# Keys loaded in two layouts and the decay moved to the values, in the attention stage of a fused attention and expert kernel

## The chip, the cores and the metric

The kernel runs on one core of one Trainium2 chip, in one launch. The metric is the device time of that launch in microseconds, the median of several runs. Its engines are named as in the profile: PE is TensorE (PEld its weight load), DVE is VectorE, ACT is ScalarE, POOL is GpSimd, and SP is SyncE, whose queue issues most transfers.

## The reference

Three layers follow each other: an attention without softmax, in which a score decays with the distance of its two positions, a choice of one of 8 experts for each token, and a dense layer with a cosine.

```python
# q, k, v: 8 batches, 8 heads, 576 positions, 64 columns, float32
scores = scale * np.matmul(q, k.transpose(0, 1, 3, 2))
gamma = 1.0 - 2.0 ** (-5.0 - np.arange(H))            # one for each head
Dmat = np.where(rel >= 0, gamma[:, None, None] ** rel[None], 0.0)   # rel = query position - key position
attn = np.matmul(scores * Dmat[None], v)              # rows of all heads side by side: x, 4608 x 512
...
logits = x @ w_gate                                   # 8 experts, the largest is taken
h = np.maximum(xe @ w1[e], 0.0); ye = h @ w2[e]       # for the tokens of each expert
...
h = x @ w_in; g = h * np.cos(h); out = g @ w_out      # 4608 x 512, 2048 wide inside
```

## The kernel before

The change lies in the attention stage, the first 180 us or so. It works through 40 steps: 8 batches, each of which is cut into 5 chunks of positions, four of 128 and a last one of 64. Since gamma to the power of a distance is a product of one power for the query and one for the key, the kernel multiplies each row of keys by gamma to the minus position (`decay_k`, tile `kp`) and each column of results by gamma to the position (the table `gx`).

Each step `i` issues, in this order: the transposes of the decayed keys of a chunk ahead (`transposes`, PE into `tp`, ACT copies them to `kpT`); the scores of chunk `i` (`scores`, PE into `sc`, DVE multiplies them by the causal mask into `pT`); the decay of the keys of chunk `i + 2` (DVE); for chunk `i - 1` the part of the result that comes from earlier chunks (`inter`, which reads the running state in `sbd`) and that from its own (`intra`, into `xps`, which DVE turns into `xt`); the update of the state S (`kp` times values, summed in PSUM, which ACT copies to `sbd`); and for chunk `i - 2` the turning of results into rows of x together with the logits (`rows`, PE into `rw`, ACT copies to `xs`, SP writes `xd`). The first chunk of a batch has no `inter`, the last one no state.

Once a batch, the routing of the batch that has just been finished runs beside this, one part a step: `route` (DVE finds the best expert), `place` (PE counts, DVE and POOL compute the slots: `dd`, `ge`, `hot`), `spread` (POOL builds `oh` and `rt`), and two steps later `table` (PE multiplies `oh` and `rt` into `lg`). Weights of the first expert are split into two parts in pieces, three pieces a batch in most batches: ACT casts a piece (`wunit`), DVE subtracts.

Nothing is scheduled by a planner: each engine runs its instructions in the order in which the code issues them, and waits where data or a buffer is missing. SP's queue holds the loads of chunk `i + 4` behind the write of x of chunk `i - 2`. Keys and values of a chunk come as one block (`ldkv`, 6 buffers), the queries, which the host has turned, as another (`ldq`, 6 buffers). The lines that matter:

```python
def decay_k(i):
    ...
    nc.vector.tensor_mul(out=kp[:n], in0=s["k"][:n], in1=g.unsqueeze(2).to_broadcast([n, H, D]))
...
mm(out=scs[g][r:r + D, j, :n], lhsT=s["kpT"][D * g:D * g + D, j, r:r + D],
   rhs=s["qT"][D * g:D * g + D, j, :n], start=(j == 0), stop=True, skip_group_check=True)
```

Of the kernel before, what the change touches and what calls it, by code (L numbers as in the profile page):

```python
# [40 lines left out]
NWARM = 16  # L41
# [62 lines left out]
def turned_queries(q):  # L104

    B, H_, S, D_ = q.shape
    t = q.reshape(B, H_ // 2, 2, S, D_).transpose(0, 2, 4, 1, 3).reshape(B, 2 * D_, H_ // 2, S)
    return np.concatenate([t[:, :, :, o:o + n].reshape(B, 2 * D_, -1) for o, n in CH], axis=2)


def rows_of_tokens(k, v):

    B, H_, S, D_ = k.shape
    return np.stack([a.transpose(0, 2, 1, 3).reshape(B * S, H_ * D_) for a in (k, v)], axis=1)
# [3 lines left out]
def attn_moe_kernel(ctx, tc, qt, kv, wg, w1, w2, win, wout, ctab, out):  # L118
    nc = tc.nc
    B = qt.shape[0]  # L120
# [233 lines left out]
    with ExitStack() as actx:  # L354
# [57 lines left out]
        halfkv = [ap1.tile([P, 2, H, D], F32, name=f"halfkv{i}") for i in range(2)]  # L412
        halfpT = ap1.tile([P, H, D], F32, name="halfpT")
        for t in [t.rearrange("p s h d -> p s (h d)")[D:, 1] for t in halfkv] + [halfpT[D:]]:
            nc.gpsimd.memset(t, 0.0)
# [5 lines left out]
        def load_q(i):  # L421
            b, c = steps[i]
            o, n = CH[c]
            t = ap3.tile([P, 4, P], F32, tag="ldq", name="ldq", bufs=6)
            nc.sync.dma_start(out=t[:, :, :n], in_=qt[b, :, 4 * o:4 * (o + n)].rearrange("p (j t) -> p j t", j=4))
            st[i]["qT"] = t

        def load_kv(i, parts=(slice(0, 2),)):
            b, c = steps[i]
            o, n = CH[c]  # L430
            if "kv" not in st[i]:
                t = st[i]["kv"] = ap3.tile([P, 2, H, D], F32, tag="ldkv", name="ldkv", bufs=6) if n == P else halfkv[b % 2]
                st[i]["k"], st[i]["v"] = t[:, 0], t[:, 1]
            for a in parts:
                nc.sync.dma_start(out=st[i]["kv"][:n, a].rearrange("p s h d -> p s (h d)"),
                                  in_=kv[b * SEQ + o:b * SEQ + o + n, a])

        def loads(i):
            load_kv(i)
            load_q(i)  # L440

        def decay_k(i):
# [8 lines left out]
        def transposes(i):  # L451
# [1016 lines left out]
```

## Time and profile before

| what | value |
|---|---|
| median of 3 runs | 1392.07 us (1389.79 to 1395.18) |
| the profiled execution | 1386.7 us |
| its span, first to last instruction | 1384.6 us |
| TensorE busy | 1368.3 us, 99% of the span |
| VectorE busy | 962.6 us, 70% |
| ScalarE busy | 703.9 us, 51% |
| GpSimd busy | 199.1 us, 14% |
| transfers | 292.22 MB, 211 GB/s on average |

The profile is of one execution, which was 3.1 us faster than the fastest of the three others; times within it are microseconds from the start of its span. A busy share is an average over stages: what a change in the attention stage does is read from that stage's rows.

### The profile page before, as it was taken

The page shows a single profiled execution, that of the slowest core. Times are in us where ns is not written, and L with a number is a line of the kernel's source. Part 1 is how long each engine was busy: PE and PEld are TensorE (multiplying, and loading weights), DVE is VectorE, ACT ScalarE, POOL GpSimd, SP SyncE. Part 2 cuts the span into 40 slices and gives each one's busy share as a digit, 9 for nine tenths or more (in the row PEclk, how much of TensorE's full clock was granted, in tenths as well). Part 3 has the DMA queues.
Part 4 walks back from the last instruction along what each step waited for, and adds up shares of the span by engine and source line. Part 5 has one row for each costly group of instructions (what it writes and reads, how often), then busy time and mean ns, then how long its engine had stood idle before and what let it go on. Part 6 is the DMA issues. An engine that isn't in the chain of part 4 may idle for free.

```text
span 1384.6 us, 28487 instructions
## 1 busy us (share of the span) xinstructions
PE 1368.3 (99%) x11401; PEld 1274.7 (92%) x11401; DVE 962.6 (70%) x1968; ACT 703.9 (51%) x1407; POOL 199.1 (14%) x300
## 2 busy tenths in 40 slices
PE   8999999999999999999999999999999999999998
PEld 7999999999999999998999999999999999999997
DVE  5888865768687786947676676666766667666655
ACT  3444434444444445435555565555555555555544
POOL 4435441021311122100010000101001010010101
PEclk9999999999999999999999999999999999999999
DMA  8878615566776577877565644646555564554551
GB/s 255 264 249 269 199 57 197 181 222 204 270 244 218 194 250 260 303 297 268 196 227 185 225 177 176 257 161 226 192 192 204 180 253 161 197 225 172 191 183 61
DMA packets 80329, 292.22 MB, mean 211 GB/s; under 512 B 12356, under 2 KB 20512, under 8 KB 69952
## 3 DMA queue, kind: packets, MB, share of 16 engines
q1 hardware_dynamic: 67680, 247.79, 51.6%
q0 software_dynamic: 12512, 42.56, 8.4%
q8 instruction: 91, 1.49, 0.4%
q14 instruction: 46, 0.38, 0.1%
HBM read 238.85 MB, written 51.47 MB: 210 GB/s over the span
## 4 chain that ended last, share of the span: by engine, by line
PE 54%; DMA 1%; POOL 0%; POOLq 0%; DVE 0%; issue 0%
PE acc L1375 28%; PE hps L1299 26%; DMA wquad<-ws 1%; POOLq L1464 0%; POOL out_dram L1357 0%; DVE orow L1353 0%; POOL spare L155 0%
## 5 line engine op out<-in xcount | busy, mean ns | idle before, releaser
L1375 PE MATMUL acc<-wunit,gh 128*128 128x512 f32 x1152 | 358.2, 392 | 0.0
L1299 PEld LDWEIGHTS hps<-far,wquad 128*128 128x128 f32 x2064 | 261.8, 191 | 9.1 <-issue 1.2
L1299 PE MATMUL hps<-far,wquad 128*128 128x256 f32 x2064 | 266.7, 283 | 1.6 <-DMA wquad<-ws 1.1
L1375 PEld LDWEIGHTS acc<-wunit,gh 128*128 128x128 f32 x1152 | 207.2, 189 | 36.0
L1375 PE MATMUL acc<-wunit,gl 128*128 128x512 f32 x576 | 224.3, 389 | 0.0
L270 PE MATMUL hps<-xT,wunit 128*128 128x256 f32 (+6 forms) x1536 | 209.5, 297 | 0.6 <-ACT yev L287 0.5
L270 PEld LDWEIGHTS hps<-xT,wunit 128*128 128x128 f32 x1536 | 206.7, 188 | 1.3 <-ACT yev L287 0.7
L285 PE MATMUL hps<-hh,wunit 128*128 128x256 f32 (+6 forms) x960 | 196.3, 299 | 0.0
L285 PEld LDWEIGHTS hps<-hh,wunit 128*128 128x128 f32 x960 | 154.6, 188 | 0.1
L285 PE MATMUL hps<-hl,wunit 128*128 128x256 f32 (+6 forms) x480 | 142.7, 297 | 1.3 <-DVE hl L274 1.3
L1357 POOL DMA_INDIRECT out_dram<-orow,perm x36 | 35.3, 981 | 739.8 <-DVE orow L1353 735.9
L1375 PEld LDWEIGHTS acc<-wunit,gl 128*128 128x128 f32 x576 | 108.2, 188 | 24.4 <-DVE gl L1342 0.8
L1336 DVE SCALAR_TENSOR_TENSOR sa<-sa,box 128x512 f32<-128x512 f32 x144 | 99.0, 687 | 42.9 <-ACT sa L1334 42.8
L1340 ACT CAST gh<-sa 128x512 fp32r<-128x512 f32 x144 | 89.5, 622 | 73.6 <-DVE sa L1336 73.6
L1299 PE MATMUL hps<-near,wquad 128*128 128x256 f32 x960 | 126.6, 283 | 0.0
L1299 PEld LDWEIGHTS hps<-near,wquad 128*128 128x128 f32 x960 | 123.1, 191 | 3.6
L1310 DVE TENSOR_TENSOR box<-hps,box 128x256 f32<-128x256 f32 x72 | 30.6, 424 | 135.9 <-PE hps L1299 135.8
L1342 DVE TENSOR_TENSOR gl<-sa,gh 128x512 fp32r<-128x512 f32 x144 | 99.0, 687 | 18.4 <-ACT gh L1340 12.9
L1331 DVE SCALAR_TENSOR_TENSOR sa<-box,ka 128x512 f32<-128x512 f32 x144 | 98.9, 687 | 12.4 <-ACT ka L1329 12.3
L1055 DVE TENSOR_TENSOR wunit<-wst,wunit 128x512 fp32r<-128x512 f32 x112 | 75.2, 686 | 37.1 <-ACT wunit L1054 36.9
L1309 ACT COPY box<-hps 128x256 f32<-128x256 f32 x72 | 26.7, 371 | 142.5 <-PE hps L1299 133.7
L1333 ACT ACTIVATE sa<-sa 128x512 f32<-128x512 f32 x144 | 91.3, 634 | 8.2 <-DVE sa L1331 8.2
(220 smaller groups left out, 1889.4 us busy)
## 6 DMA issues: line engine op xcount, KB each, us to landing
wquad<-ws SPq DMA_DIRECT2D x72, 1792.0 KB, 7.2
wst<-in_moe_w_dram SPq DMA_DIRECT2D x64, 512.0 KB, 5.0
ldkv<-in_kv_dram SPq DMA_DIRECT2D x28, 512.0 KB, 4.4
ws<-cvo POOLq DMA_DIRECT2D x28, 512.0 KB, 4.2
ldq<-in_qt_dram SPq DMA_DIRECT2D x32, 256.0 KB, 4.4
xd<-xs SPq DMA_DIRECT2D x32, 256.0 KB, 2.4
cvw<-in_moe_w_in_dram SPq DMA_DIRECT2D x16, 512.0 KB, 4.5
cvw<-in_moe_w_out_dram SPq DMA_DIRECT2D x16, 512.0 KB, 4.4
```

The lines of the kernel that those rows point to most:

```text
L270: mm(out=ph[:, :n], lhsT=u[:, a, kc, f0:f0 + P], rhs=t[:, bq, kc, :n], start=(idx == 0), stop=(idx == 11))
L285: mm(out=py[:, :n], lhsT=u[:, w], rhs=t[:, :n], start=(fc == 0 and g == 0), stop=(fc == 7 and g == 2))
L1055: nc.vector.tensor_sub(out=u[:, 1, 2 * g + c], in0=s[:, c], in1=u[:, 0, 2 * g + c])
L1299: mm(out=o, lhsT=u[:, s, kc, a], rhs=x[:, bq, kc], start=(s in (0, 1, 2) and idx == 0), stop=(idx == 5), skip_group_check=True)
L1310: nc.vector.tensor_add(out=u2, in0=y[:, :HT], in1=p1)
L1331: nc.vector.scalar_tensor_tensor(out=sa, in0=x, scalar=INV2PI, in1=ka, op0=ALU.mult, op1=ALU.subtract)
L1333: nc.scalar.activation(out=sa, in_=sa, func=AF.Sin, scale=math.pi)
L1336: nc.vector.scalar_tensor_tensor(out=sa, in0=sa, scalar=-1.0, in1=x, op0=ALU.add, op1=ALU.mult)
L1340: nc.scalar.copy(out=gh, in_=sa)
L1342: nc.vector.tensor_sub(out=gl, in0=sa, in1=gh)
L1357: ins = nc.gpsimd.indirect_dma_start(out=out[:, :], out_offset=bass.IndirectOffsetOnAxis(ap=perm[:, k:k + 1], axis=0), in_=o, in_offset=None)
L1375: mm(out=acc2[T][c], lhsT=pair[n][:, fh, c % 2 * P:(c % 2 + 1) * P], rhs=u[:, w, fc % 4], start=(q == 0 and fh == 0 and n == 0 and w == 0) ...
```

## The change

The host lays the inputs of the attention out anew. For each chunk there is one block: keys turned, queries turned, rows of values, rows of keys, 2 KB of each for every partition, so 8 KB for a partition and 1 MB for a full chunk (`full`). A half chunk has its turned keys and queries in one block (`part`) and its values in another (`tail`); its rows of keys aren't loaded, since nothing reads them. Keys are thus loaded twice, and neither multiplied nor turned on the chip. The decay goes onto the values: eight ACT multiplications a chunk, one for each head, each by a column of one number for a partition (`decay`, tile `vs`), issued one step ahead rather than two. The scores read the turned keys as loaded, the state is the product of plain keys and decayed values.

The bank of PSUM that held the transposes becomes a fourth buffer of `sc`. Blocks have 5 buffers (`ld`). The first loads stand in another order, the warm-up matmuls go from 16 + 4 to 13, and the rows that the first expert gathers get 3 buffers of their own and are turned in `sc`.

```diff
-        def decay_k(i):
+        def decay(i):
             b, c = steps[i]
             o, n = CH[c]
             s = st[i]
-            kp = ap3.tile([P, H, D], F32, tag="kp", name="kp", bufs=4)
-            g = cc(C_GK + c * H, H, n)
-            nc.vector.tensor_mul(out=kp[:n], in0=s["k"][:n], in1=g.unsqueeze(2).to_broadcast([n, H, D]))
-            s["kp"] = kp
-
-        def transposes(i):
...
-            for j in range(4):
-                nc.tensor.transpose(pt[:, j, :n], s["kp"][:n, 2 * j:2 * j + 2, :].rearrange("p a d -> p (a d)"),
-                                    ident[:n, :n])
-            t = ap3.tile([P, 4, P], F32, tag="kpT", name="kpT")
-            nc.scalar.copy(out=t[:, :, :n], in_=pt[:, :, :n])
-            s["kpT"] = t
+            vs = ap3.tile([P, H, D], F32, tag="vs", name="vs", bufs=4) if n == P else halfv[b % 2]
+            for h in range(H):
+                nc.scalar.mul(vs[:n, h], s["v"][:n, h], cc(C_GK + c * H + h, 1, n))
+            s["vs"] = vs
...
+        def load(i, *parts):
...
+            if "ld" not in s:
+                t = s["ld"] = ap3.tile([P, 4, 4 * P], F32, tag="ld", name="ld", bufs=5)
...
+            if n == P:
+                for a0, a1 in parts or ((0, 4),):
+                    nc.sync.dma_start(out=t[:, a0 * 512:a1 * 512], in_=full[b, c, :, a0 * 512:a1 * 512])
+            else:
+                nc.sync.dma_start(out=t[:, :8 * n], in_=part[b])
+                nc.sync.dma_start(out=s["ld"][:n, 2], in_=tail[b])
...
-                        mm(out=scs[g][r:r + D, j, :n], lhsT=s["kpT"][D * g:D * g + D, j, r:r + D],
+                        mm(out=scs[g][r:r + D, j, :n], lhsT=s["kT"][D * g:D * g + D, j, r:r + D],
...
-                mm(out=xp[r:r + D, k, :n], lhsT=s["v"][:, h, :], rhs=s["pT"][:, h, :n],
+                mm(out=xp[r:r + D, k, :n], lhsT=s["vs"][:, h, :], rhs=s["pT"][:, h, :n],
...
-                    mm(out=sps[r:r + D, h // 2, :], lhsT=s["kp"][:, h, :], rhs=s["v"][:, h, :],
+                    mm(out=sps[r:r + D, h // 2, :], lhsT=s["k"][:, h, :], rhs=s["vs"][:, h, :],
...
+        load(0, (0, 2))
         nc.sync.dma_start(out=ca[:, :C_TRI - C_MASK], in_=ctab[:, C_MASK:C_TRI])
+        load(0, (2, 3))
+        load(1, (0, 2))
+        nc.sync.dma_start(out=gx[:, 0].rearrange("p j t -> p (j t)"), in_=ctab[:, C_GX:])
+        load(0, (3, 4))
+        load(1, (2, 4))
+        load(2, (0, 2))
         nc.sync.dma_start(out=ct, in_=ctab[:, :C_MASK])
...
+        load(2, (2, 4))
+        load(3)
...
-            if i < LEAD:
-                transposes(i + 1)
-            if i + 2 < NS:
-                decay_k(i + 2)
+            if i + 1 < NS:
+                decay(i + 1)
...
-                loads(i + 4)
+                load(i + 4)
```

The order in which the engines find their instructions changes at three places on which the prediction rests. The first is TensorE, from the transposes ahead of the last chunk of a batch to the table of the batch before; `sc` are scores, `xps` first the part from the state (`sbd`) and then the chunk's own (`pT`), `S` the state, `rw` the rows of x, `lg` the table's product. Before:

```order
L457 MATMUL tp<-ct,kp 128x128 x4
L473 MATMUL sc<-ldq,kpT 64x64 x8
L498 MATMUL xps<-ldq,sbd_137 64x128 x8
L508 MATMUL xps<-pT,ldkv 64x128 x8
L517 MATMUL S<-ldkv,kp 64x64 x8
L529 MATMUL rw<-wgi,xt_132 128x136 x4
L457 MATMUL tp<-ct,kp 128x128 x4
L473 MATMUL sc<-ldq,kpT 64x128 x16
L498 MATMUL xps<-ldq,sbd_136 64x64 x8
L508 MATMUL xps<-halfpT,halfkv_143 64x64 x8
L648 MATMUL lg<-rt,oh 128x120 x5
```

And the same place after the change:

```order
L462 MATMUL sc<-ld 64x64 x8
L487 MATMUL xps<-ld,sbd_137 64x128 x8
L497 MATMUL xps<-pT,vs 64x128 x8
L506 MATMUL S<-vs,ld 64x64 x8
L518 MATMUL rw<-wgi,xt_132 128x136 x4
L462 MATMUL sc<-ld 64x128 x16
L487 MATMUL xps<-ld,sbd_136 64x64 x8
L497 MATMUL xps<-halfpT,halfv_143 64x64 x8
L637 MATMUL lg<-rt,oh 128x120 x5
```

The transposes are gone, and the table's matmuls stand where they stood; so there is less TensorE work between the start of a batch's routing on GpSimd and the matmuls that need it. The second place is ScalarE, in the two steps of a batch that cast weights (the last chunk's, and the first one's of the next batch). Before:

```order
L460 COPY kpT<-tp 128x512
L761 CAST wunit<-wst 128x512
L520 COPY sbd_136<-S 128x256
L531 COPY xs<-rw 128x256 x2
L460 COPY kpT<-tp 128x512
L761 CAST wunit<-wst 128x512 x2
L531 COPY xs<-rw 128x256 x2
```

After:

```order
L729 CAST wunit<-wst 128x512
L449 ACTIVATE vs<-ld,ca 128x64 x8
L509 COPY sbd_136<-S 128x256
L520 COPY xs<-rw 128x256 x2
L729 CAST wunit<-wst 128x512 x2
L449 ACTIVATE vs<-ld,ca 128x64 x8
L520 COPY xs<-rw 128x256 x2
```

One copy of keys has become eight multiplications of values, ahead of the copies of the state and of x. The third place is ScalarE at the start of the kernel. Before:

```order
L460 COPY kpT<-tp 128x512 x3
L520 COPY sbd_136<-S 128x256
L460 COPY kpT<-tp 128x512
L520 COPY sbd_137<-S 128x256
L531 COPY xs<-rw 128x256 x2
```

After:

```order
L449 ACTIVATE vs<-ld,ca 128x64 x24
L509 COPY sbd_136<-S 128x256
L449 ACTIVATE vs<-ld,ca 128x64 x8
L509 COPY sbd_137<-S 128x256
L520 COPY xs<-rw 128x256 x2
```

The decays of chunks 0, 1 and 2 (24 multiplications), each of which waits for its values, now stand ahead of the first copy of the state.

## Rows read from the trace of the kernel before

**Rows 1.** The page, part 1: busy time, share of the span, instructions.

```profile
PE 1368.3 (99%) x11401; PEld 1274.7 (92%) x11401; DVE 962.6 (70%) x1968; ACT 703.9 (51%) x1407; POOL 199.1 (14%) x300
```

**Rows 2.** Windows, one batch: busy time by engine, then clock, DMA share, GB/s.

```profile
52.81:74.42 21.61, 21.61 (x425) 19.59 (x424) 18.50 (x52) 9.53 (x24) 9.35 (x14) 1.00 0.75 246
```

**Rows 3.** Timeline of TensorE: start, duration of the group, line, tiles, count.

```profile
18.71 1.10 PE L473 MATMUL sc<-ldq,kpT 64*64 64x128 f32 x32
19.64 0.61 PE L498 MATMUL xps<-ldq,sbd 64*64 64x128 f32 x16
...
22.70 0.60 PE L457 MATMUL tp<-ct,kp 128*128 128x128 f32 x4
23.23 0.62 PE L473 MATMUL sc<-ldq,kpT 64*64 64x64 f32 x14
...
72.02 0.91 PE L648 MATMUL lg<-rt,oh 128*128 128x120 f32 x5
...
169.36 0.46 PE L457 MATMUL tp<-ct,kp 64*128 64x64 f32 x4
169.75 1.10 PE L473 MATMUL sc<-ldq,kpT 64*64 64x128 f32 x32
...
174.27 0.62 PE L473 MATMUL sc<-ldq,kpT 64*64 64x64 f32 x13
```

**Rows 4.** Timeline of ScalarE, then groups by form (busy us, mean ns).

```profile
86.27 0.37 ACT L520 COPY sbd<-S 128x256 f32<-128x256 f32 x1 [2.60 <-PE S L517]
...
87.76 0.58 ACT L460 COPY kpT<-tp 128x512 f32<-128x512 f32 x1
...
169.71 1.32 ACT L242 ACTIVATE xrow<-xrow,gateE 128x512 f32<-128x512 f32 x2
...
L255 ACT CAST xT<-tp 128x512 fp32r<-128x512 f32 x30 | 16.3, 594 | 0.2
...
L255 ACT CAST xT<-tp 128x256 fp32r<-128x256 f32 x1 | 0.4, 374 | 0.0
```

**Rows 5.** Timeline of GpSimd and VectorE around a batch's routing.

```profile
62.07 0.52 POOL L586 TENSOR_TENSOR dd<-dsts,ca 128x200 f32<-128x200 f32 x1 [11.84 <-DVE dsts L580]
...
64.17 1.16 POOL L594 TENSOR_TENSOR hot<-hot,ge 128x200 f32<-128x200 f32 x1
64.18 0.67 DVE L448 TENSOR_TENSOR kp<-ldkv,ca 128x512 f32<-128x512 f32 x1
...
66.92 3.55 POOL L623 TENSOR_SCALAR oh<-ca,rm 128x128 fp32r<-128x128 f32 x5
...
70.31 0.68 DVE L785 TENSOR_TENSOR wunit<-wst,wunit 128x512 fp32r<-128x512 f32 x1
...
71.33 0.52 POOL L637 TENSOR_TENSOR rt<-hot,gl 128x200 fp32r<-128x200 f32 x1
...
172.40 0.61 POOL L594 TENSOR_TENSOR hot<-hot,ge 128x200 f32<-128x200 f32 x1
...
176.14 2.93 POOL L623 TENSOR_SCALAR oh<-ca,rm 128x128 fp32r<-128x128 f32 x5 [1.51 <-DVE gts L629]
```

**Rows 6.** Timeline of VectorE at the start: decays that waited for keys.

```profile
7.13 0.69 DVE L448 TENSOR_TENSOR kp<-ldkv,ca 128x512 f32<-128x512 f32 x1 [2.36 <-DMA ldkv<-in_kv_dram]
...
12.88 0.81 DVE L448 TENSOR_TENSOR kp<-ldkv,ca 128x512 f32<-128x512 f32 x1 [1.16 <-DMA ldkv<-in_kv_dram]
```

**Rows 7.** Transfers: 10 to 14 us; 40 to 160 us; issues (count, KB, us to landing).

```profile
DMA packets 850, 1.53 MB, mean 383 GB/s; under 512 B 132, under 2 KB 132, under 8 KB 850
...
DMA packets 15441, 31.02 MB, mean 258 GB/s; under 512 B 4015, under 2 KB 4015, under 8 KB 15416
...
ldkv<-in_kv_dram SPq DMA_DIRECT2D x23, 512.0 KB, 4.5
...
wquad<-ws SPq DMA_DIRECT2D x72, 1792.0 KB, 7.2
...
wunit<-wd SPq DMA_DIRECT2D x8, 1024.0 KB, 9.0
```

More of the change, by code (lines that the diff above doesn't have):

```diff
@@ L40 @@
 MAXOVB = 40
-NWARM = 16
+NWARM = 13
 INV2PI = 1.0 / (2.0 * math.pi)
@@ L101, in const_table, with of_chunks, turned, rows @@
     return t.astype(np.float32)
-def turned_queries(q):
+def of_chunks(q, k, v):
     B, H_, S, D_ = q.shape
[L107 to L114, printed above, removed]
+    def turned(x, o, n):
+        t = x[:, :, o:o + n].reshape(B, H_ // 2, 2, n, D_).transpose(0, 2, 4, 1, 3)
+        return t.reshape(B, 2 * D_, H_ // 2 * n)
+    def rows(x, o, n):
+        return x[:, :, o:o + n].transpose(0, 2, 1, 3).reshape(B, n, H_ * D_)
+    full = np.stack([np.concatenate([turned(k, o, n), turned(q, o, n), rows(v, o, n), rows(k, o, n)], axis=2)
+                     for o, n in CH[:-1]], axis=1)
+    o, n = CH[-1]
+    return full, np.concatenate([turned(k, o, n), turned(q, o, n)], axis=2), rows(v, o, n)
 @with_exitstack
-def attn_moe_kernel(ctx, tc, qt, kv, wg, w1, w2, win, wout, ctab, out):
+def attn_moe_kernel(ctx, tc, full, part, tail, wg, w1, w2, win, wout, ctab, out):
     nc = tc.nc
-    B = qt.shape[0]
+    B = full.shape[0]
     NT = B * SEQ
@@ L419, in attn_moe_kernel @@
         st = [dict() for _ in steps]
[L421 to L440, printed above, removed]
-        def decay_k(i):
+        def load(i, *parts):
             b, c = steps[i]
@@ L467, in scores @@
             pT = ap2.tile([P, H, P], F32, tag="pT", name="pT") if n == P else halfpT
-            scs = [ps1.tile([P, 4, P], F32, tag="sc", name="sc", bufs=3) for g in range(2)]
+            scs = [ps1.tile([P, 4, P], F32, tag="sc", name="sc", bufs=4) for g in range(2)]
             for j in range(4):
@@ L743, in attn_moe_kernel @@
         nc.vector.memset(idle, 0.0)
-        blank = ps1.tile([P, 8, P], F32, tag="x", name="xps").rearrange("p a t -> p (a t)")
-        warm(NWARM, blank, idle)
-        decay_k(0)
-        transposes(0)
-        warm(NWARM // 4, blank, idle)
-        decay_k(1)
-        LEAD = 3
+        warm(NWARM, ps1.tile([P, 8, P], F32, tag="x", name="xps").rearrange("p a t -> p (a t)"), idle)
+        decay(0)
         wq = dict(zip((6, 7, 11, 15, 16, 21, 25, 26), [(key, g) for key in w_units(0) for g in range(2)]))
@@ L1451 @@
     arrays, args = {}, []
-    laid = {"qt": turned_queries(inputs['q']), "kv": rows_of_tokens(inputs['k'], inputs['v'])}
-    for name in ["qt", "kv"] + _INS:
+    laid = dict(zip(("full", "part", "tail"), of_chunks(inputs['q'], inputs['k'], inputs['v'])))
+    for name in ["full", "part", "tail"] + _INS:
         a = np.ascontiguousarray(laid.get(name, inputs.get(name)))
```

44 lines of the change are left out of this document (12 added, 32 removed).

## The prediction, made before the result was known

> **What bounds the kernel now.** I read the page first: TensorE is busy for 99% of the span [rows 1]. Then the table of windows, cut at the batches of the attention stage: one batch takes 21.61 us, TensorE is busy for all of it, VectorE for 18.50, ScalarE for 9.53, GpSimd for 9.35, and the DMA engines for 0.75 of it [rows 2]. So TensorE sets the pace, VectorE has 3 us to spare, ScalarE 12. The timeline of TensorE shows what fills a batch: the transposes of one full chunk start at 22.70 and the scores behind them at 23.23, so they hold TensorE for 0.53 us; those of a 64-token chunk start at 169.36, the scores at 169.75, 0.39 us [rows 3]. After the stage TensorE goes on without a pause into the experts, whose first blocks hang on the stage's end; so I take a microsecond won in the stage as one won at the end.
>
> **What the change removes.** Between the start of scores of step 3 (18.71) and that of the last step (174.27) stand the transposes of chunks 5 to 39, 35 of them [rows 3]: seven batches of four full chunks and a half one. 28 x 0.53 + 7 x 0.39 = 17.57 us of TensorE's time go. A batch would then take 21.61 - (4 x 0.53 + 0.39) = 19.10 us, if nothing else holds it. Whatever stands before 18.71 is a matter of arrivals, below. VectorE loses 40 multiplications of 0.67 us, which costs nothing and frees it; ScalarE loses the copy of the turned keys, 0.58 us for a full chunk [rows 4].
>
> **What it puts on ScalarE.** Eight multiplications of 128x64 a step. No such row exists, so I bound it: a multiplication by a column of gates of 128x512 is the nearest in kind; two of them in a row take 1.32 us at 0.71 each, so the second costs 0.61 [rows 4]. Casts of 512 and 256 columns take 594 and 374 ns, 0.86 ns a column [rows 4]; 448 columns less make 0.71 into 0.33 and 0.61 into 0.23. So eight cost between 8 x 0.23 = 1.8 us (overlapping as the pair does, and nothing speaks against that) and 8 x 0.33 = 2.65 (not overlapping). I take 1.9. Does it hide? In a plain step ScalarE waits 2.60 us before it copies the state S [rows 4] and did the keys' copy of 0.58 before; a step gets 0.53 shorter, so there is room for 2.60 + 0.58 - 0.53 = 2.65 us, and 1.9 fits. In a step with one weight cast (0.5 more) it still fits; the step with two casts copies no state. By the sum of a batch: 9.53 - (4 x 0.58 + 0.37) + 5 x 1.9 = 16.3 of 19.10 us. So it costs nothing on the path. The Trainium skill (ScalarE: Activation LUTs, Rules for kernel authors) says to do a multiplication on VectorE, not on ScalarE; the rows agree on the instruction's price (one of 0.67 us there against 1.9 here), but not on the kernel's, because the cheaper engine is the one with less room. By the rule the step should lengthen, by the row of waits it doesn't.
>
> **Who is late next.** GpSimd. Once a batch it works through the routing of the batch before: from the first subtraction at 62.07 to the end of the last product at 71.33 + 0.52 = 71.85 without a gap, 9.78 us, and TensorE starts the table's matmuls that read them at 72.02 [rows 3, 5]. So there was at most 0.17 us to spare. Three transposes (0.39 + 0.53 + 0.53 = 1.45 us) leave TensorE's road between the two, so it arrives 72.02 - 62.07 - 1.45 = 8.50 us after GpSimd starts. With GpSimd as it was, TensorE would wait 9.78 - 8.50 = 1.28 to 1.45 us in each of six batches, 7.7 to 8.7 us. But GpSimd was held up: its product `hot` takes 1.16 us at 64.17, while VectorE multiplies keys from 64.18 to 64.85, and 0.61 at 172.40, when there are no more keys; its five comparisons take 3.55 us at 66.92, the next multiplication of keys falling among them, and 2.93 at 176.14 [rows 5]. Those multiplications go, so the chain shortens by 0.55 + 0.62 to 8.6 us. What stays is a collision with the weights' subtraction on VectorE (70.31), which may land on another operation [rows 5]. I take a wait of 0.3 us a batch, bounds 0 and 0.6: 1.8 us, 0 to 3.6. The Trainium skill (SBUF — State Buffer, Who interferes with whom) has the same thing as a rule: a VectorE instruction with two inputs in SBUF and a GpSimd instruction that reads SBUF exclude each other for a whole instruction. The pairs of rows agree with it, and by the rule ScalarE's multiplications would not hold GpSimd up at all, which gives the same 1.8 us; without the rule it would be the 7.7 to 8.7.
>
> **The start.** Before, the second chunk's keys were there at 7.13 with 1.00 MB asked for (three blocks of 0.262 MB and 0.21 MB of constants), the fourth's at 12.88 with 2.83 MB (seven blocks more) [rows 6]: 318 GB/s. In the list of ScalarE after the change the decays of chunks 0, 1 and 2 all stand ahead of the first copy of S, so that copy, and with it the second step, waits for the values of chunk 2, which lie 3.62 MB deep in the queue. At that pace they come at 7.13 + 2.62/0.318 = 15.4, at the 383 GB/s of 10 to 14 us [rows 7] at 14.0, and perhaps 1 us sooner, since rows of 4 KB now go ahead of the small constants. Then 1.9 (decay), 0.4 (copy) and 3.06 of TensorE's work (in step 3 from 19.64 to 22.70 [rows 3]) to the scores of step 3: 18.4 to 20.8, against 18.71. I take 19.4: a loss of 0.7 us (gain of 0.3 to loss of 2.1). The fewer warm-up matmuls cost nothing where TensorE waits for data; the granted clock was 1.00 (2.4 GHz) in the batch shown [rows 2], and if it falls to 1.2 GHz in the new gaps, a first step of 3 us takes 3 us more.
>
> **The transfers.** A full chunk loads 1.05 MB in place of 0.79, so a batch moves 5.77 MB (its rows of x included) in 19.10 us, 302 GB/s, and 357 with two weight units. Before, the mean was 258 GB/s, with 4,015 packets under 512 B (mostly the half chunks' queries), which go [rows 7]. A full queue moved 383 GB/s [rows 7]. So the pace suffices: nothing on the path, with 7% to spare in the worst batches. One block of 1 MB lands later than two small ones: 512 KB took 4.5 us [rows 7], another 0.52 MB at 383 GB/s make 5.9. It is issued about 1.0 us into the step after the one that frees its slot (behind a write of x on SP's queue), and ScalarE reads it two steps later, 0.55 us in; it can bear some 1.5 us more before its copy of S is late. A step lasts 19.10/5 = 3.82: 2 x 3.82 + 0.55 - 1.0 + 1.5 = 8.7 us. That holds.
>
> **The sum.** 17.57 - 1.8 - 0.7 = 15.1 us. The profiled execution took 1386.7 us and would take 1371.6. It lies below all three runs (1389.79 to 1395.18), whose median is 1392.07; from there, 1377.0. That is what I predict for the median.
>
> **The rivals.**
> - GpSimd's chain is not relieved (the slow operations were slow for another reason). For it: 0.17 us to spare, and GpSimd's times are rough. Against: both slow operations coincide with a multiplication of keys. 17.57 - 8.2 - 0.7 = 8.7 us won, 1383.4.
> - ScalarE becomes the bound, if short multiplications don't overlap: a weight batch holds 9.53 - 2.69 + 5 x 2.65 = 20.1 us of work against 19.10. There are 16 casts, three a batch, so 5.3 such batches; at least 1.0 us each, and 1.8 if its other short operations stop overlapping too, make 5.3 to 9.5 us given back: 7 to 12 won, about 1383. Against it: the pair at 1.32 us.
> - Slower: the 1 MB block lands late. Five slots and a load that waits for a slot make a ring. With L from issue to landing, a step can't be shorter than (L - 1.05)/2. From 8.7 us on it costs; at 2 x 4.32 + 1.05 = 9.7 us the step is as long as before, and beyond, the kernel is slower: at 10.5 us a step takes 4.73, 36 steps lose 14.6 us, 1407. For it: 1024 KB blocks of another stage took 9.0 us [rows 7]; against: 1792 KB took 7.2 [rows 7], and this stage's own loads 4.5. If it comes at 9.2 us, a step takes 4.08 and (4.32 - 4.08) x 36 = 8.6 us are won: 1383.
> - TensorE's clock falls at the start: 3 us more, 1380.
>
> **Numbers.** Forecast 0.62 (own range 1371 to 1381), GpSimd 0.13, ScalarE 0.09, late blocks 0.12 (0.05 of it slower than before), clock 0.04. Range 1371 to 1385: from the full 17.57 and a start that gains, with the runs' own scatter of some 2 us, up to the first two rivals. About 0.5% (7 us) is what a measurement can tell from no change: faster 0.87, same 0.08, slower 0.05 (some of the late blocks and the worst of ScalarE's and GpSimd's cases end within 7 us).
>
> **What the profile after would show.** A batch of 19.1 to 19.7 us in place of 21.61; eight ScalarE multiplications in 1.9 us; `hot` at 0.61 us and the comparisons at 2.9; a small pause of TensorE ahead of the table's matmuls, once a batch; scores of step 3 at 18.4 to 20.8. I am wrong if the copy of S waits for ScalarE's own queue rather than for TensorE in plain steps, if decays wait for `ld` beyond the start, or if the table's matmuls wait over 1 us.

## The result and the profile after

The changed kernel took 1378.75 us (median of 6 runs, 1377.49 to 1384.35) against 1392.87 us for the kernel before in the same series (6 runs, among them the three shown above): a ratio of 0.9911, 95% interval 0.9892 to 0.9930. A second series (e5 below) gave 1381.42 against 1389.41 us, 0.9936 (0.9923 to 0.9950). So it is faster, by 0.6 to 0.9%, 8 to 14 us; the forecast was 1377.0.

The profiled execution of after took 1377.58 us. From its page, span and busy time of each engine, which answer to [rows 1]:

```profile
span 1375.3 us, 28314 instructions
...
PE 1354.1 (98%) x11234; PEld 1262.5 (92%) x11234; DVE 939.5 (68%) x1928; ACT 757.2 (55%) x1687; POOL 191.0 (14%) x300
```

TensorE's work shrank by 14.2 us (1368.3 to 1354.1), the span only by 9.3, and TensorE is idle for longer: some of what was taken off its road became waiting. The windows of three batches (each from the scores of a second chunk to the next) answer to [rows 2]; columns are busy time and instruction count of each engine, granted clock, DMA share and rate:

```profile
core 0: us, PE busy (x) PEld busy (x) DVE busy (x) ACT busy (x) POOL busy (x), PEclk, DMA share, GB/s
51.59:74.36 22.77, 20.30 (x405) 17.98 (x405) 15.90 (x49) 17.08 (x65) 8.03 (x14) 1.00 0.89 305
113.64:133.32 19.68, 19.68 (x405) 17.75 (x405) 15.65 (x47) 16.31 (x59) 8.24 (x14) 1.00 0.97 354
133.32:152.82 19.50, 19.50 (x407) 17.70 (x406) 16.44 (x54) 15.15 (x57) 8.43 (x15) 1.00 0.89 313
```

An undisturbed batch takes 19.50 us in place of 21.61, with TensorE busy throughout. One batch takes 22.77, longer than before, with TensorE idle for 2.47 of it. The timeline of TensorE shows where it waits, with the idle time before an instruction and its releaser in brackets (compare [rows 3]):

```profile
9.88 1.98 PE L462 MATMUL sc<-ld 64*64 64x128 f32 x32 [3.44 <-DMA ld<-in_full_dram]
...
18.02 0.67 PE L487 MATMUL xps<-ld,sbd 64*64 64x128 f32 x16 [2.68 <-ACT sbd L509]
...
21.23 1.10 PE L462 MATMUL sc<-ld 64*64 64x128 f32 x32
...
60.85 0.39 PE L506 MATMUL S<-vs,ld 128*64 128x64 f32 x6 [1.67 <-issue]
...
72.40 0.91 PE L637 MATMUL lg<-rt,oh 128*128 128x120 f32 x5 [0.25 <-POOL rt L626]
...
116.17 1.19 PE L518 MATMUL rw<-wgi,xt 128*128 128x136 f32 x8
117.29 0.97 PE L462 MATMUL sc<-ld 64*64 64x128 f32 x25
```

In the kernel before, the rows of x ahead of the transposes at 22.70 ([rows 3]) stand there as

```profile
21.67 1.19 PE L529 MATMUL rw<-wgi,xt 128*128 128x136 f32 x8
```

The timeline of ScalarE in the kernel after (compare [rows 4]):

```profile
8.51 1.28 ACT L449 ACT_TABLE_LOAD   x1 [8.51 <-DMA ld<-in_full_dram]
9.81 2.02 ACT L449 ACTIVATE vs<-ld,ca 128x64 f32<-128x64 f32 x8
12.79 2.02 ACT L449 ACTIVATE vs<-ld,ca 128x64 f32<-128x64 f32 x8 [0.97 <-DMA ld<-in_full_dram]
15.69 2.02 ACT L449 ACTIVATE vs<-ld,ca 128x64 f32<-128x64 f32 x8 [0.88 <-DMA ld<-in_full_dram]
17.62 0.35 ACT L509 COPY sbd<-S 128x256 f32<-128x256 f32 x1
...
60.46 2.02 ACT L449 ACTIVATE vs<-ld,ca 128x64 f32<-128x64 f32 x8 [3.57 <-DMA ld<-in_full_dram]
```

Four things are to be seen. Scores of step 3 start at 21.23 us, 2.5 later than before, because the copy of S stands behind the decay of chunk 2, which waits for its block until 15.69. In the loop ScalarE waits up to 3.57 us for a block, and TensorE pauses for 1.67 us in the middle of sixteen equal matmuls. Scores start 1.12 us behind the rows of x (116.17 to 117.29), where the transposes started 1.03 behind them (21.67 to 22.70). And GpSimd is quicker (compare [rows 5]); its timeline:

```profile
65.99 0.61 POOL L583 TENSOR_TENSOR hot<-hot,ge 128x200 f32<-128x200 f32 x1
...
68.20 2.94 POOL L612 TENSOR_SCALAR oh<-ca,rm 128x128 fp32r<-128x128 f32 x5
```

Between scores of step 3 and those of the last step lie 144.68 us in place of 155.56; the last step's scores come at 165.91 in place of 174.27, 8.4 us earlier. That is the gain that the two profiles show for the stage.

### The profile page after: what moved, and what is told of

It is laid out like the page before. It is cut to its first block, busy times and chain, and to the rows that moved or that the text cites. A ratio compares the mean times of both kernels' runs of the same rounds, so it can differ in the third digit from the quotient of the medians.

```text
span 1375.3 us, 28314 instructions
## 1 busy us (share of the span) xinstructions
PE 1354.1 (98%) x11234; PEld 1262.5 (92%) x11234; DVE 939.5 (68%) x1928; ACT 757.2 (55%) x1687; POOL 191.0 (14%) x300
## 4 chain that ended last, share of the span: by engine, by line
PE 49%; issue 6%; POOL 0%; POOLq 0%; ACT 0%
PE acc L1341 25%; PE hps L1265 24%; POOL out_dram L1323 0%; POOLq L1430 0%; ACT ka L1295 0%; POOL spare L159 0%; PE acc L1352 0%; POOLq L1323 0%; ACT orow L1321 0%
```

## The experiments

Theory, from these rows: the change is worth some 15 us in TensorE's time, of which 2.5 are lost at the start to ScalarE's order and 4 to 5 in the loop to blocks that land late; GpSimd is relieved because VectorE's multiplication is gone. Rivals: the clock or the transfers make the start; the stalls are chance; GpSimd's times have another reason. The table has what each profile shows (us; starts of scores), and the times; "e1" is the number in the name of the run below.

| kernel | step 3 | last step | between | time | ratio to before |
|---|---|---|---|---|---|
| before | 18.71 | 174.27 | 155.56 | 1392.87 | |
| e1, before again | 19.38 | 175.53 | 156.15 | 1388.29 (one run) | |
| after | 21.23 | 165.91 | 144.68 | 1378.75 | 0.9911 (0.9892 to 0.9930) |
| e5, after again | 22.23 | 167.45 | 145.22 | 1381.42 | 0.9936 (0.9923 to 0.9950) |
| e2, start's order | 18.92 | 161.40 | 142.48 | 1377.01 | 0.9910 (0.9888 to 0.9933) |
| e3, start's clock | 21.18 | 165.14 | 143.96 | 1380.93 (one run) | |
| e4, early weights | 22.60 | 165.25 | 142.65 | 1379.39 | 0.9929 (0.9903 to 0.9954) |
| e6, e2 and e4 | 18.94 | 163.55 | 144.61 | 1377.63 | 0.9912 (0.9898 to 0.9925) |
| e7, decay on VectorE | 23.70 | 176.22 | 152.52 | 1390.54 | 1.0004 (0.9989 to 1.0019) |
| e8, transposes back | 22.98 | 181.61 | 158.63 | 1397.69 | 1.0058 (1.0043 to 1.0074) |
| e9, no rows of keys | 19.25 | 159.33 | 140.08 | not comparable | |
| e11, e2 and split blocks | 18.98 | 159.80 | 140.82 | 1375.29 | 0.9894 (0.9872 to 0.9916) |
| e12, before, more traffic | 19.64 | 177.58 | 157.94 | 1391.84 | 1.0014 (1.0002 to 1.0026) |

**e1, the kernel before once more** (nothing edited).

> The kernel before, unchanged, profiled a second time. Its profiled execution took 1386.7 us and lay 6 us under the median of its own runs (1392.87 us), that of the kernel after 1377.58 us, 1 us under its median (1378.75 us). So the two profiles show 9.1 us between the kernels and the medians 14.1. If the profiled execution of before was simply a quick one, a second profile lies nearer to 1390 us, with the same 21.6 us a batch in the attention stage and the difference spread over the stages behind it. If the attention stage itself varies from execution to execution, its batches or its start differ from those of the first profile (scores of step 3 at 18.71, of the last step at 174.27 us).

It took 1388.29 us. The stage ends 1.3 us later, what lies behind it varies hardly: from scores of the last step to the end of the span 1210.3 and 1210.7 us. So the quick profile of before was no outlier of the stage, and the 14.1 us between the first medians aren't in the traces.

**e5, the kernel after once more** (nothing edited).

> The kernel after, unchanged, profiled and timed again beside the next three kernels. The two profiles of before agree within 1.3 us up to the scores of the last step (174.27 and 175.53 us) and within 0.4 us behind them; both show 21.6 us a batch. If the stall of 3.27 us in one batch of the first profile of after (51.59 to 74.36 us) belongs to the kernel, it stands here again, in the same batch; if it is chance, it stands elsewhere or is smaller, and undisturbed batches still take 19.5 us. The start (scores of step 3 at 21.23 us) should come again within 1.5 us, since ScalarE's order makes it. The time: 0.989 to 0.993 of before.

The stalls stand elsewhere, but cost nearly the same: 145.22 us between the marks against 144.68. So the place of a stall is chance. Its size isn't fixed either: the loop behind step 3 is the same code in e2 and e3, and takes 142.48 and 143.96 us there. The timeline of TensorE has the pause of 1.6 us again, now ahead of the sixth last matmul of the rows of x, and the view of transfers (30 to 145 us; count, size and median from issue to landing) gives the block 8.8 us:

```profile
86.46 0.96 PE L518 MATMUL rw<-wgi,xt 128*128 128x136 f32 x6 [1.64 <-issue]
```

```profile
ld<-in_full_dram SPq DMA_DIRECT2D x23, 1024.0 KB, 8.8
xd<-xs SPq DMA_DIRECT2D x23, 256.0 KB, 5.3
```

The start is 1.0 us later, although the copy of S came at 17.03: the granted clock stood at 0.66 and 0.50 (the 1.2 GHz level) between 18 and 22 us, and the rows of x there took 2.08 us in place of 1.19. From the matmuls that waited for the copy of S to scores of step 3 lie 4.80 us, in the first profile 3.21 (18.02 to 21.23):

```profile
17.43 0.67 PE L487 MATMUL xps<-ld,sbd 64*64 64x128 f32 x16 [1.77 <-ACT sbd L509]
...
22.23 1.10 PE L462 MATMUL sc<-ld 64*64 64x128 f32 x32
```

Behind the last step's scores lie 1211.8 us, in the first profile 1209.4. The two pairs of profiles agree on 8.4 and 8.1 us for the stage; the second pair of medians on 8.0.

**e2, the order at the start.**

```diff
-            if i + 1 < NS:
+            if 3 <= i < NS - 1:
                 decay(i + 1)
...
                 inter(i - 1)
                 intra(i - 1)
+            if i < 3:
+                decay(i + 1)
```

> Only the place of the decay in the first three steps differs from the kernel after: the decay of chunk i + 1 is issued behind the step's copy of S instead of ahead of it. Theory: at the start ScalarE's own order holds TensorE up. The first copy of S stands behind the decay of chunk 2, which waits for values that are 3.6 MB deep in the queue, until 17.6 us. Then with this edit the copy of S comes at about 15 us, behind the decay of chunk 1 alone, scores of step 3 start at 18.4 to 19.0 us in place of 21.23, and the kernel takes 2.2 to 2.8 us less (1376 us). Rival: the transfers or TensorE's clock (0.50 to 0.69 of full speed from 10 to 14 us) set the start; then scores of step 3 stay at 20.5 to 21.3 us and the time doesn't move by more than 0.7 us.

The theory holds for the start. ScalarE's timeline, then TensorE's:

```profile
13.94 0.35 ACT L509 COPY sbd<-S 128x256 f32<-128x256 f32 x1
```

```profile
15.04 0.67 PE L487 MATMUL xps<-ld,sbd 64*64 64x128 f32 x16 [0.51 <-DVE xt L500]
...
18.92 1.10 PE L462 MATMUL sc<-ld 64*64 64x128 f32 x32 [0.60 <-DMA ld<-in_full_dram]
```

The copy of S comes 3.7 us earlier, TensorE no longer waits for it, and scores of step 3 start 2.3 us earlier, now held by a block. The time doesn't show it: the ratio is 0.9910, that of after 0.9911. In the profiles the stage ends 4.5 us earlier than in the first one of after (161.40), 2.3 of them from the start and 2.2 from the loop, but what lies behind took 1212.8 us in place of 1209.4.

**e3, the clock at the start.**

```diff
+            if i == 1:
+                warm(18, ps1.tile([P, 8, P], F32, tag="x", name="xps").rearrange("p a t -> p (a t)"), idle)
             scores(i)
```

> Adds work that computes nothing: 18 more warm-up matmuls of 128x256 in TensorE's wait of 3.44 us ahead of the scores of step 1, from 6.4 us on. Theory: in the kernel after TensorE's clock falls there (granted 0.50 in 10 to 12 us, 0.69 in 12 to 14), which costs the scores of step 1 and the first products some 1.7 us, but this lies beside ScalarE's wait for the values of chunk 2, so scores of step 3 still start at 21.2 us and the time stays. Rival: the clock sets the start; then scores of step 3 start at 19.5 us. If the added matmuls don't keep the clock up, the windows of 10 to 14 us show it and the run tells nothing on the rest.

The windows show that the clock stayed up (0.50 and 0.69 in after):

```profile
10.00:12.00 2.00, 2.00 (x43) 1.42 (x43) 0.29 (x1) 0.76 (x4) 2.00 (x5) 1.00 1.02 376
12.00:14.00 2.00, 2.00 (x62) 1.87 (x56) 2.00 (x7) 1.26 (x6) 2.00 (x5) 1.00 1.05 422
```

Scores of step 3 start at 21.18 us all the same, but not by the road that the expectation had. The values of chunk 2 landed earlier here (the decay starts at 14.05), so the copy of S came at 15.97 and TensorE went on 1.65 us earlier than in after; then the clock fell a second time, to 0.50, and this took the 1.6 us back:

```profile
16.37 0.67 PE L487 MATMUL xps<-ld,sbd 64*64 64x128 f32 x16 [2.19 <-ACT sbd L509]
...
21.18 1.10 PE L462 MATMUL sc<-ld 64*64 64x128 f32 x32
```

```profile
18.00:20.00 2.00, 2.00 (x24) 1.88 (x23) 0.69 (x1) 1.48 (x7) 0.47 (x1) 0.50 0.93 358
```

So the time of 21.18 by itself tells nothing on the first fall. That it cost nothing is read from the waits: 2.68 us for the copy of S in after, which itself followed ScalarE's wait for values. The second fall does cost. From the matmuls behind that wait to scores of step 3 take 4.80 or 4.81 us in e3, e4, e5, e8 and e10, where the granted clock fell to between 0.50 and 0.57 in one of the 2 us windows there, and 3.21 in the first profile of after alone, where it stayed at 1.00.

**e4, early weights, and e6, both edits.**

```diff
-        wq = dict(zip((6, 7, 11, 15, 16, 21, 25, 26), ...
+        wq = dict(zip((2, 3, 11, 15, 16, 21, 25, 26), ...
```

> Only the steps differ in which the first two weight blocks of 512 KB are asked for: 2 and 3 (at some 20 us, where the transfer engines are half used) in place of 6 and 7 (at 37 and 42 us, where the queue is full). Theory: in the one batch of 22.77 us ScalarE waits 3.57 us for a chunk's block, which takes 10.9 us to land because the queue is loaded with more than the 320 to 365 GB/s that it moves. With the weights asked for earlier that wait goes or falls under 1 us, the batch takes 19.5 to 20 us, and scores of the last step start some 3 us earlier (at 163 us in place of 165.91). Rival: a block of 1 MB lands late whatever else is in the queue, five slots are too few, and the stall of about 3 us stays or moves to the neighbouring batch; then scores of the last step stay within 1 us of 165.9.

> Both earlier edits together: the decays of the first three steps behind the copy of S, and the first two weight blocks asked for in steps 2 and 3. Theory: scores of step 3 at about 19 us (2.3 earlier than after), no batch over 20.5 us, scores of the last step at 160 to 162 us in place of 165.9, and a time 3 to 5 us below that of the kernel after beside it. Rival: what the attention stage gains is given back behind it, where TensorE waits for VectorE in the experts (6.7 us of such pauses in the profile with the first edit, 4.2 in that of the kernel after); then the last step's scores come early and the time stays within 2 us of after.

Neither theory came out whole. In e4 the batch that took 22.77 us takes 19.48, but a step in another batch takes 5.57 us in place of 3.65, with a pause of 1.65 us again. What that pause is, the next section tells. In e6 the start comes at 18.94, but then the early batch, which now has the weights in its queue, loses it: 22.80 us from 29.81 to 52.61, with TensorE waiting 1.11 and 0.40 us for the copy of S. In e4 the wait of 3.57 us for a block went with the weights (the longest is 2.1); in e6 a block comes late where they went to (3.4). e6's gain over e5, 3.9 us in the stage and 3.8 in the median, wasn't given back behind the stage (1210.3 us there).

**e7, the decay on VectorE.**

```diff
-            for h in range(H):
-                nc.scalar.mul(vs[:n, h], s["v"][:n, h], cc(C_GK + c * H + h, 1, n))
+            g = cc(C_GK + c * H, H, n)
+            nc.vector.tensor_mul(out=vs[:n], in0=s["v"][:n], in1=g.unsqueeze(2).to_broadcast([n, H, D]))
```

> The decay of the values is one VectorE multiplication a chunk, two inputs in SBUF, in the place of the eight ScalarE ones; nothing else changes. Theory of the prediction: such a multiplication holds GpSimd up. Then `hot` takes about 1.15 us again in place of 0.61, the five comparisons 3.5 in place of 2.93, GpSimd's chain about 9.7 us, and TensorE waits 1.2 to 1.5 us for it ahead of the table's matmuls in each of six batches: the kernel is 7 to 9 us slower than after (scores of the last step at 172 to 174 us), if each multiplication falls on the same operations. Rival: GpSimd's times have to do with something else that the change took away; then `hot` stays at 0.61, the table's matmuls wait under 0.4 us, and the kernel takes as long as after, or less, because ScalarE has less to do at the start.

GpSimd's groups by line (30 to 165 us; busy time and mean ns), and TensorE's timeline:

```profile
L612 POOL TENSOR_SCALAR oh<-ca,rm 128x128 fp32r<-128x128 f32 x30 | 24.6, 835 | 0.0
L583 POOL TENSOR_TENSOR hot<-hot,ge 128x200 f32<-128x200 f32 x6 | 6.9, 1151 | 0.5
```

```profile
95.06 0.91 PE L637 MATMUL lg<-rt,oh 128*128 128x120 f32 x5 [1.94 <-POOL rt L626]
```

`hot` is back at 1151 ns and five comparisons take 4.2 us (835 ns each; 601 in e5). The table's matmuls wait 0.89, 0.82, 1.94, 1.94, 1.94 and 1.06 us, 8.6 in all, and the median lies 9.1 us above e5's, beside which it ran (8.8 in the stage, by the scores of the last step). In the batch shown `hot` starts at 86.46 and VectorE's multiplication of values at 86.47. The price that the prediction gave its first rival, 8.2 us, is about what the change avoids. The Trainium skill (SBUF — State Buffer, Who interferes with whom) has the rule: a VectorE instruction with two inputs in SBUF and a GpSimd instruction that reads SBUF shut each other out for a whole instruction; this run agrees, 1151 against 610 ns. Its advice to multiply on VectorE (ScalarE: Activation LUTs, Rules for kernel authors) would have cost those 9.1 us here.

**e8, the transposes back.** They turn rows of values, from chunk 5 on; `sc` has three banks again.

```diff
+        def turns_again(i):
+            n = CH[steps[i][1]][1]
+            pt = ps1.tile([P, 4, P], F32, tag="tp", name="tp")
+            for j in range(4):
+                nc.tensor.transpose(pt[:, j, :n], ...)
...
+            if 4 <= i < NS - 1:
+                turns_again(i + 1)
             scores(i)
```

> Adds work that nothing reads: from step 4 on, four transposes of 128x128 on TensorE ahead of each step's scores, where the kernel before had them, into a bank taken from the four of `sc` (three are left, as before). Theory of the prediction: they hold TensorE for 0.53 us a full chunk, 17.6 us in all, and a plain batch takes 19.50 + 2.51 = 22.0 us. Rival, from the trace of after: the scores now start 0.1 us later behind the rows of x than the transposes did, so a full chunk's transposes were worth 0.43 us; then a batch takes 21.6 us and the last step's scores come 14.8 us later (181 us). A third: a bank less for `sc` makes a new wait; then the batch is longer than 22.1 us.

```profile
123.02 1.19 PE L525 MATMUL rw<-wgi,xt 128*128 128x136 f32 x8
124.05 0.60 PE L456 MATMUL tp<-ct,ld 128*128 128x128 f32 x4
124.58 1.10 PE L469 MATMUL sc<-ld 64*64 64x128 f32 x32
```

The first rival is right. Transposes still stand 0.53 us ahead of the scores (TensorE's timeline), but they start 1.03 us behind the rows, so the scores lie at 1.56 where after has 1.12: a difference of 0.44. The plain steps are 4.08, 4.63, 4.52, 4.10 and 4.28 us, 21.61 in all, the batch of before; in after they are 3.65, 4.24, 4.08, 3.66 and 3.85, 19.48. So the 35 groups of transposes are worth 7 x 2.13 = 14.9 us and not 17.57.

**e9, no rows of keys.**

```diff
-                for a0, a1 in parts or ((0, 4),):
+                for a0, a1 in parts or ((0, 3),):
...
-                    mm(out=sps[r:r + D, h // 2, :], lhsT=s["k"][:, h, :], rhs=s["vs"][:, h, :],
+                    mm(out=sps[r:r + D, h // 2, :], lhsT=s["v"][:, h, :], rhs=s["vs"][:, h, :],
```

> Leaves out the rows of keys: a full chunk's block is 768 KB in place of 1 MB, and the state is the product of the plain values (in place of keys) and the decayed values, with the same instructions. Theory: the second copy of the keys costs the attention stage what the trace of after shows as stalls between scores of step 3 and of the last step (144.7 and 145.2 us in its two profiles, where seven batches of 19.48 us and a step's rest would make 140.7), because the transfer engines run full; and part of the late start. Then this kernel shows 140.7 to 141.5 us there, no pause of TensorE over 0.6 us, scores of step 3 at 20 us or earlier, and a time 4 to 6 us below after. Rival: the stalls come from the number of instructions or from chance; then they stand here too (144 us or more).

The later layers work on other values here, so only the stage is compared. It shows no pause of TensorE of 0.25 us or more between 10 us and the last step's scores, 140.08 us between the marks, and a start at 19.25. The block (transfers, 30 to 145 us) lands 2.7 us sooner:

```profile
ld<-in_full_dram SPq DMA_DIRECT2D x24, 768.0 KB, 6.1
```

So against the two profiles of after the second copy of the keys costs 4.6 and 5.1 us in the loop (less the waits for GpSimd, 0.5 and 0.9, which are gone here too) and 2.0 and 3.0 at the start. Against e2 and e3, with the same loop, it is 2.4 and 3.9.

**e10, ScalarE's work doubled.**

```diff
+                for _ in range(1 + (i > 4)):
-                nc.scalar.mul(vs[:n, h], s["v"][:n, h], cc(C_GK + c * H + h, 1, n))
+                    nc.scalar.mul(vs[:n, h], s["v"][:n, h], cc(C_GK + c * H + h, 1, n))
```

> Adds work: from step 4 on each of ScalarE's eight multiplications is issued twice, so a step holds 3.9 us of them in place of 2.0. The prediction says that a plain step has room for 2.65 us and that 1.9 of it is used. Then 1.9 us more exceed the room by 1.1 to 1.2 us in the three steps of a batch that copy a state, some 24 steps, and the attention stage takes 25 to 30 us longer. Rival: ScalarE, busy for 16.3 of 19.5 us a batch by the prediction's sum, has room only as a batch's total; then 16.3 + 5 x 1.9 = 25.8 us is what a batch takes, 6.3 us longer, 44 us in all. If it costs under 15 us, the engine had more room than the prediction gave it.

It took 1452.86 us (one run), 71 more than e5. ScalarE's timeline and the window of a batch:

```profile
93.75 5.09 ACT L450 ACTIVATE vs<-ld,ca 128x64 f32<-128x64 f32 x16
```

```profile
92.33:122.58 30.25, 23.43 (x404) 20.17 (x404) 15.55 (x47) 28.92 (x99) 7.77 (x14) 0.89 0.68 226
```

Both numbers expected are too low, for one reason: sixteen take 5.08 us and not 3.9, 0.32 apiece in place of 0.25; the second of a pair reads and writes what the first did. So a batch got 5 x 3.06 = 15.3 us more of it and 10.75 us longer: ScalarE had some 4.5 us to spare, about what the plain batch of after shows (19.50 - 15.15 = 4.35). This is rough: TensorE's clock stood at 0.89 in that window, and ScalarE was still idle for 1.33 us. But ScalarE is the bound (28.92 of 30.25 us), and it is the batch's total that counts, as the rival has it.

**e11, the start's order and split blocks.** Beside e2's edit:

```diff
-                for a0, a1 in parts or ((0, 4),):
+                for a0, a1 in parts or ((0, 3), (3, 4)):
```

> The edit of the start (decays of the first three steps behind the copy of S) and, from chunk 3 on, a full chunk's block as two transfers, 768 KB with the turned keys, the queries and the values first, and 256 KB of key rows behind. The bytes stay. Theory: ScalarE's decay then waits for three quarters of the block alone, so that its waits for blocks in the loop fall by about a quarter of 8 to 11 us, and the stalls of 2 to 4.5 us in the stage shrink to under 1.5; scores of step 3 at about 19 us, of the last step at 160 to 161, the time 4 to 6 us below after (0.989 to 0.991 of before). Rival: the queue's pace, not what stands first in it, makes the stalls, and one more issue on SP's queue delays what follows; then scores of the last step come at 162 us or later, as with the edit of the start alone (161.4).

Transfers (30 to 145 us), the window of a batch, and ScalarE's waits (22 to 165 us; total, times, longest):

```profile
ld<-in_full_dram SPq DMA_DIRECT2D x24, 768.0 KB, 6.6
...
ld<-in_full_dram SPq DMA_DIRECT2D x24, 256.0 KB, 7.2
```

```profile
108.39:127.89 19.50, 19.50 (x405) 17.68 (x404) 15.85 (x47) 16.41 (x59) 8.23 (x14) 1.00 0.99 354
```

```profile
ACT vs L449 <- DMA ld<-in_full_dram: 5.7, 8, 1.4
```

With the same bytes, at a DMA share of 0.99, the loop takes 140.82 us, within 0.8 of e9, and TensorE shows no pause of 0.25 us or more in it. In after the same row of waits says

```profile
ACT vs L449 <- DMA ld<-in_full_dram: 13.6, 12, 3.6
```

So it isn't the bytes as such: with the same bytes the stalls go when the values, which are needed first, needn't land with the whole megabyte. How much the split is worth is less sure: after's loop took 144.68 and 145.22 us, but e2 and e6, which share this kernel's order at the start, 142.48 and 144.61. So it is 1.7 to 4.4 us, by one profile of e11. The kernel takes 1375.29 us, clearly less than before; its 0.9894 (0.9872 to 0.9916) lies below e5's 0.9936 (0.9923 to 0.9950), but overlaps with the first series of after and with e2.

**e12, more traffic in the kernel before.** 256 KB more for each full chunk from chunk 4 on, to a place in device memory that nothing reads.

```diff
             load_kv(i)
             load_q(i)
+            if CH[steps[i][1]][1] == P:
+                nc.sync.dma_start(out=junk[i * P:(i + 1) * P, :]..., in_=kv[steps[i][0] * SEQ:steps[i][0] * SEQ + P, 0:1])
```

> The kernel before with more work: with each full chunk from 4 on 256 KB more are moved, from the rows of keys to a place in device memory that nothing reads, on SP's queue behind the chunk's own blocks. Theory: traffic alone makes stalls of the kind that after shows (ScalarE or VectorE late for a block, TensorE pausing for nothing that the profile shows). Then the stage from scores of step 3 to those of the last step, 155.6 and 156.2 us in the two profiles of before, takes 2 to 5 us longer. Rival: before has room, since its blocks are asked for four steps ahead into six buffers; then it stays within 1 us of 156, and the stalls of after belong to its five buffers and its 1 MB blocks.

1.8 to 2.4 us more between the marks, the low end of what the theory allowed. VectorE's and TensorE's timelines:

```profile
71.36 0.69 DVE L451 TENSOR_TENSOR kp<-ldkv,ca 128x512 f32<-128x512 f32 x1 [1.96 <-DMA ldkv<-in_kv_dram]
```

```profile
72.19 0.63 PE L460 MATMUL tp<-ct,kp 128*128 128x128 f32 x4 [1.27 <-DVE kp L451]
```

Traffic alone makes stalls of one kind, an engine late for its block. TensorE's pauses for nothing that the profile shows don't appear.

## Why the prediction held, and where it didn't

The time came within 2 us of the forecast, but the sum behind it was 6.7 us too high: 15.1 against 8.4 in the stage. What made up for it is that the forecast stood on the median of the runs of before, and the first series showed 14.1 us between the medians, of which the traces and the second series (8.0) show 8. That is luck. For the profiled execution the same sum said 1371.6, and it took 1377.58; from the second series' 1389.41 it would have said 1374.3, against 1381.42. What the change removes and what bounds the kernel held; one cost was put at nothing and wasn't, and three sizes were off.

- **What bounds the kernel** and **what goes on with the stage's end**: right. What lies behind the last step's scores took 1209.4 to 1213.6 us in before, after, their repeats and e2 to e4 and e6, so the stage's gain is the kernel's.
- **The transposes, 17.57 us**: mis-sized; 14.9 (e8). The prediction took the distance from transposes to scores (0.53) for what goes, and not that scores behind the rows start 0.09 to 0.10 us later than transposes do.
- **ScalarE hides the decay**: right in what it costs, 2.02 us for eight against 1.9, 15.2 to 16.3 us busy a batch against 16.3; e10 gives it some 4.5 us of room. But the picture of a step was wrong, and two of the prediction's own signs of being wrong are there: decays wait for `ld` all through the loop (13.6 us), and most copies of S stand behind ScalarE's own work. Of 27 copies in the kernel before all waited for TensorE, of 29 in after only 10 (lines below). It costs nothing as long as TensorE needs the copy later still: it waited for one in the loop once in e5 (0.54 us) and never in after.
- **GpSimd, 1.8 us lost**: the mechanism right (e7), the size 0.5 us in the first profile (two waits of 0.25) and 0.9 in the second (0.62 and 0.25), in two of six batches and not in each.
- **The start, 0.7 us lost**: mis-sized; 2.5 and 2.9, beyond its bound of 2.1. The chain named was right (e2), but the values of chunk 2 came at 15.69 in after, beyond the slow end of 14.0 to 15.4, where the prediction took the quick one (15.10 in e5, 14.05 in e3). The clock did fall, as one rival had it: the first fall lay beside the wait for the copy of S, a second one behind it cost 1.6 us in e3, e4, e5, e8 and e10, half of what the rival said. That the first profile of after was spared it is chance, as far as is known.
- **The transfers, nothing on the path**: the step that failed. The prediction let a block land in 5.9 us, the time of a block by itself at a full queue's pace, and named 8.7 us as the point from which it costs. In the median blocks take 8.8 us in e5 and 7.3 to 8.1 in e2, e4, e6, e7 and e8; single ones take up to 10.9 (after, issued at 49.49, read by ScalarE at 60.46). Against e9's loop without pauses the cost is 4.6 and 5.1 us, GpSimd's waits included. In part it is the rival of the late blocks, at its mild end. In part it is one that the prediction didn't have: TensorE's own code came late, a pause of 1.67 us in after and of 1.64 in e5 (below). In after the two overlap: ScalarE's decay started at 60.46, so TensorE would have waited for part of that time anyway.

ScalarE's waits for TensorE ahead of copies of S (22 to 165 us; total, times, longest), in before and then in after:

```profile
ACT sbd L520 <- PE S L517: 57.5, 27, 2.6
```

```profile
ACT sbd L509 <- PE S L506: 5.9, 10, 1.0
```

Summed up: 155.56 - 140.08 = 15.5 us won between the marks without pauses (14.9 by batches; the rest are small waits of before), 4.6 given back in the loop, 2.5 at the start: 8.4. Of the 4.6 TensorE's idle time shows 3.0; the rest lies in steps that take longer while TensorE counts as busy.

What TensorE's pauses of 0.9 to 1.7 us are, which the profile lays to nothing ("issue"), the traces show too: TensorE had run out of code. The pauses stand once in each of five profiles of kernels with 1 MB blocks in the loop (after, e3 to e6), not in the other four (e2, e7, e8, e10), and in none with smaller blocks (before, e1, e9, e11, e12). They fall between equal matmuls of one group, which wait for no new data. TensorE's code comes over a DMA queue of its own, q8 in the view of transfers, in blocks of 16 KB: 89 blocks for the 22,663 instructions that the trace of after has of TensorE, some 255 in each. In after such a block starts at 49.5 us, none from 50 to 58.2, and the next right ahead of the pause (the two stretches, 50 to 58.2 and 58.2 to 59.2):

```profile
q1 hardware_dynamic: 778, 2.75, 91.8%
```

```profile
q1 hardware_dynamic: 87, 0.23, 129.5%
q8 instruction: 1, 0.02, 6.7%
```

From the records of the traces, times in us; the last column counts TensorE's instructions, weight loads and waits included, ahead of the one that goes on:

| kernel | code block before starts | this one, from to | pause of TensorE | instructions |
|---|---|---|---|---|
| after | 49.5 | 58.3 to 59.4 | 59.18 to 60.85 | 1985 |
| e5 | 76.3 | 84.1 to 85.1 | 84.82 to 86.46 | 3009 |
| e3 | 59.3 | 69.1 to 70.0 | 69.91 to 71.36 | 2497 |
| e4 | 124.6 | 133.1 to 134.0 | 133.61 to 135.26 | 5057 |
| e6 | 123.5 | 131.3 to 132.2 | 132.70 to 133.56 | 5057 |

Each pause ends 1.2 to 1.5 us behind the landing of a code block, and the counts differ by multiples of 256: TensorE stops where one block of code ends and the next isn't there. In these five places the block landed when TensorE had none left to that end (in e6 nine); in the nine profiles without such a pause, by the same count, at least 41 were left, 88 in e9, and 105 and 98 in before and e1. The Trainium skill (Runtime: NRT & Kernel Launch, Instruction fetch mechanics) says that an engine fetches its code in blocks by a DMA queue of its own; these traces agree.

What is still open: why those blocks of code started late. Their own transfer took 0.9 to 1.1 us, no longer than that of others; that they stood behind the 1 MB blocks fits the kernels in which they came late, and isn't shown. Nor is it shown what the sixth buffer is worth that before had and after has not; no run tries it. But e11 keeps the five and loses 0.7 us in the loop against e9.

## What to carry to other kernels

When a removed instruction stood between two of different shape, price it by the starts of what stays (row to row, step to step), not by its own duration. When transfers grow, ask how late a block lands behind what else is in the queue, and send what is needed first as a transfer of its own: with the same bytes, split 3 to 1, the loop took 140.8 us in place of 142.5 to 145.2. When an engine pauses for nothing that the profile names, look whether a block of its code landed just before it went on. Issue a wait for far-off data behind the work that is due sooner, at the start above all, and keep VectorE's operations with two inputs away from a GpSimd chain that TensorE waits for.

## What the runs showed of the hardware that was not expected

- Scores in tiles of 64x64 start 1.12 us behind the first of eight 128x128 matmuls, transposes of 128x128 only 1.03 (after, e8). The cause wasn't tried.
- The load of ScalarE's function table (1.28 us) waits with the first instruction that needs it: it stood at 8.51 us, behind the wait for the block, and came when the data was there.
- 128x64 multiplications on ScalarE follow each other every 0.24 us when they write different columns, and every 0.32 when each second one reads and writes what the one before did (e10). The cause wasn't tried.
- A queue at a DMA share of 0.97 to 0.99 moved 354 GB/s over a batch (after, e11), less than the 383 GB/s over 4 us of [rows 7].
- TensorE stops where a block of its code is late: up to 1.7 us, and it went on 1.2 to 1.5 us behind the block's landing (after, e3 to e6).
